# A gated pair of two-dimensional Fourier filters: a new order list, with twelve even sums moved to VectorE, late weights behind the last even F2 and seven even read-backs in a run

## Chip, cores and metric

The kernel runs on one core of a Trainium2 chip. The metric is the device time of one execution in microseconds (us). Before the change the median of three runs is 117.16 us (117.07 to 117.44).

## What is computed

The input `x` is 2048 x 1024 (S x D, bf16). Two filters A and B, each given by a real and an imaginary weight matrix of 2048 x 513, are applied in the frequency domain, and a gate for each row mixes the two results:

```python
def _A_ref(x, w_r, w_i):
    X = rfft2(x)
    X = X * (w_r + 1j * w_i)
    return irfft2(X, s=(S, D)).astype(bfloat16)
...
g = sigmoid((x * gate_w).sum(-1, keepdims=True))
a = _A_ref(x, A_w_r, A_w_i)
b = _B_ref(x, B_w_r, B_w_i)
return g * a + (1 - g) * b
```

## The kernel before

All transforms are matrix products with constant tables, and the work is cut into many small steps. Frequencies along D are split by parity: "even" units are n = 0 to 7 and "odd" units n = 8 to 15. The order of all work on all engines is written out by hand, as one list of tokens in the string `ORDER`; a token names a step, its indices, and the engine (A = ScalarE, D = VectorE, P = GpSimd, S = a transfer issued by SyncE) or, for TensorE steps, the PSUM bank (0 to 7). Each engine works through its own tokens in the order of the list; what one engine must wait for on another (data, a free PSUM bank, a free buffer) is found from the tiles that the steps touch. The last lines of the body are the whole driver:

```python
order = [tok.split(":") for tok in ORDER.split()]
for t in order:
    fn[t[0]](*t[1:])
```

The stages, with their tokens:

- `x`, `c`, `W`: loads of the input, of constants and of the weights of a unit (16 loads of 512 KB). Weights 0 to 7 lie in the tile `ro`, 8 to 11 in `wx`, and 12 to 15 in the even half of `y`, so those four must wait until the last even F2 has read `y`.
- `F1:s:par`: a first transform of input slice s (16 slices), for even (e) or odd (o) outputs; 8 matmuls. Its result is folded (sum and difference of two halves) into `y`: either `FC` copies one half to a buffer and `FD` adds and subtracts on VectorE (24 folds, line 382), or `FX` copies both and `FP` does it on GpSimd (8 folds). The buffers (`tmp`) are a ring of eight in `wx`.
- `F2:n:tt` (4 matmuls), its copy `T`; `F3:n` (12 matmuls), its copy `X`; `P:n:r`, the product with the weights on VectorE (two halves r of 2048 elements a lane, line 494); `Y`, `NA`, `N`: a small patch of one column of the even units, by TensorE and VectorE.
- `GH`, `GC`, `GT`, `GK`, `GZ`, `GS`: the gate, from GH's 32 matmuls to a sigmoid. `GW` then makes two gated tables from it in blocks of 4 (0, 4, 8, 12), with two VectorE instructions a block: `EA` = EA x E and `EB` = E - EA (lines 439 and 440).
- `J:n` (32 matmuls), copied by `R:n:r` to one of five `rl` buffers and stored by `H:n:tt` to a scratch in DRAM. `L:par:v` reads it back transposed, 512 KB each: `L:0` needs all of the even units' stores, `L:1` all of the odd units' stores. The read-backs go into `re` and `ro`.
- `V:par:v:s` (8 matmuls with EA and EB), its copy `VC`, and then for the even units `C:0:v:s` (4 matmuls). The result is copied by `EX` to a `tmp` buffer and its two halves added (h = 0) and subtracted (h = 1) by `EQ:v:s:h` into f32 rows in `re` (line 615); for unit 3, `E` copies the result as it is. For the odd units `U` (or `C:1:3`) makes the odd part, and output rows are the sum and the difference of both: `OR` on VectorE (line 635), or `OC` and `OP` by ScalarE and GpSimd (line 631), or for unit 3 `QD` and `QP` (lines 642 and 647). `S:v` stores the finished rows, whole units of 512 KB or halves.

Where a helper makes the copies, all have one line: 204 on ScalarE, 206 on VectorE.

SyncE issues all loads and stores but two, in the order of the list. A transfer that has to wait holds back all that stand behind it.

Of the kernel before, what the change touches and what calls it, by code (L numbers as in the profile page):

```python
# [10 lines left out]
P = 128  # L11
S = 2048
# [9 lines left out]


ORDER = """
warm:8 c:A:F1 c:A:gws tab:A x:S:0:1 x:S:1:1 x:S:2:2 x:S:4:2 x:S:6:2 x:S:8:2 x:S:10:2 x:S:12:2 x:S:14:2 c:S:FD:0:1
F1:1:o:0 F1:1:e:1 FX:1:o:D F1:0:o:2 FC:1:e:D F1:0:e:3 FP:1:o FD:1:e F1:3:o:0 F1:2:e:4 FC:0:e:D F1:3:e:1 gc:P FD:0:e
F1:2:o:5 FC:3:e:A FC:2:e:D F1:4:e:3 FD:3:e FX:2:o:A F1:5:o:6 FX:0:o:A FD:2:e F1:5:e:5 FC:4:e:A FP:0:o FX:3:o:A FD:4:e
F1:6:e:1 FC:5:e:A F1:4:o:2 FD:5:e FC:6:e:A F1:7:e:0 FP:2:o c:S:WF:0:4 FD:6:e F1:6:o:3 W:S:0 FC:7:e:A F1:9:e:7 FD:7:e
FX:6:o:A F1:8:e:1 FP:3:o FC:9:e:D c:S:WJ:0:4 F1:11:e:3 FD:9:e F1:10:e:0 c:S:w0 FC:11:e:A F1:7:o:4 c:S:PM FC:8:e:A
FP:6:o FD:11:e FX:5:o:A c:S:EZ F1:13:e:5 FC:10:e:A FD:8:e W:S:1 F1:12:e:6 FP:5:o FD:10:e c:S:WF:4:16 FC:12:e:A  # L30
F1:14:e:1 FC:13:e:A FD:12:e FX:4:o:A F1:15:e:3 W:S:2 F1:15:o:0 FD:13:e FP:4:o FC:15:e:A F1:11:o:2 FC:14:e:A FD:15:e
FC:15:o:A F1:8:o:6 c:S:WJ:4:16 F1:14:o:5 FD:14:e FC:8:o:A F1:10:o:3 neg:A:0:4 FD:15:o FC:14:o:A F1:12:o:7 FX:7:o:A
F2:0:0:1 FD:8:o c:S:E FC:10:o:A FP:7:o FC:12:o:A F2:1:0:0 W:S:3 FD:14:o T:0:0:A F2:0:1:4 FC:11:o:A F2:1:1:6 FD:10:o
T:1:0:A W:S:4 pw:P F1:13:o:1 T:1:1:A FD:12:o F1:9:o:0 T:0:1:A F3:1:5 FD:11:o c:S:FD:1:2 FC:9:o:A F3:0:3 FC:13:o:A
FD:9:o X:1:A W:S:5 F2:3:1:2 FD:13:o F2:2:0:7 X:0:A F2:3:0:0 P:1:0 W:S:6 Y:1:1 F2:2:1:5 T:3:0:A Y:0:3 neg:A:4:16 GH:4
P:1:1 W:S:7 T:2:0:A T:2:1:A NA:1:D N:1:D P:0:0 T:3:1:A GC:A NA:0:D P:0:1 F3:2:0 F2:4:0:5 X:2:A F2:4:1:2 F3:3:6 J:1:3:0
T:4:0:D T:4:1:A X:3:A P:2:0 Y:2:2 GT:0:5 R:1:0:A F2:5:0:6 Y:3:7 NA:2:D P:2:1 T:5:0:A H:1:0 F3:4:2 c:S:IG R:1:1:A
GT:1:5 W:S:8 F2:5:1:4 N:0:D NA:3:D P:3:0 X:4:A J:0:6:0 W:S:9 T:5:1:A H:1:1 N:2:D GT:2:5 P:3:1 R:0:0:A Y:4:2 GT:3:5
F3:5:3 W:S:10 R:0:1:A N:3:D H:0:0 F2:7:1:6 GK:D NA:4:D P:4:0 F2:6:1:2 X:5:A GZ:0:0 F2:6:0:5 P:4:1 GS:0 W:S:11 F2:7:0:7
T:7:0:A T:7:1:D J:2:3:0 T:6:0:A GW:D:4 T:6:1:A Y:5:6 GW:D:0 R:2:0:A N:4:D NA:5:D P:5:0 R:2:1:A H:2:0 W:S:12 H:0:1  # L40
P:5:1 F3:7:6 J:3:2:4 X:7:A H:2:1 F3:6:0 R:3:0:A F2:8:0:6 X:6:D F2:8:1:7 R:3:1:A F2:9:0:2 Y:7:3 T:8:0:D Y:6:0 T:8:1:A
GZ:1:4 NA:6:D T:9:0:A P:7:0 J:4:6:0 GS:1 F2:9:1:2 N:5:D P:7:1 R:4:0:A T:9:1:A H:4:0 P:6:0 J:5:4:6 W:S:13 R:4:1:A H:3:0
NA:7:D N:7:D R:5:0:A H:4:1 P:6:1 F3:8:2 F3:9:0 R:5:1:A F2:11:1:4 X:8:D F2:10:0:5 X:9:A H:5:1 F2:10:1:6 H:3:1 N:6:D
F2:11:0:7 W:S:14 P:8:0 T:10:0:A J:6:2:0 T:11:0:A T:11:1:A T:10:1:D R:6:0:A P:8:1 J:7:4:6 R:6:1:A H:6:0 F3:10:2 H:5:0
P:9:0 R:7:0:A P:9:1 R:7:1:A H:7:0 J:8:0:4 X:10:A GW:D:12 H:7:1 F2:12:0:6 H:6:1 F2:12:1:7 W:S:15 R:8:0:A T:12:0:D
P:10:0 R:8:1:A J:9:2:0 P:10:1 T:12:1:A H:8:1 F3:11:4 H:8:0 R:9:0:A F2:13:1:6 X:11:D R:9:1:A H:9:0 F3:12:2 F2:14:0:7
X:12:A H:9:1 F2:13:0:0 L:0:0 F2:14:1:1 L:0:1 T:13:0:A T:13:1:D P:11:0 L:0:2 J:10:4:2 L:0:3 T:14:0:A P:11:1 T:14:1:A
F3:13:6 R:10:0:A P:12:0 X:13:A H:10:0 J:11:0:4 L:0:4 P:12:1 R:10:1:A F3:14:6 R:11:0:A X:14:D F2:15:0:2 F2:15:1:3
T:15:0:A P:13:0 T:15:1:A J:12:0:6 R:11:1:A V:0:0:1:2 P:13:1 R:12:0:A F3:15:4 V:0:0:0:3 R:12:1:D X:15:A H:12:0
V:0:1:0:0 H:10:1 V:0:1:1:1 L:0:5 VC:0:1:0:A P:14:0 H:11:0 J:13:4:6 VC:0:0:0:A VC:0:1:1:A P:14:1 VC:0:0:1:A R:13:0:A  # L50
P:15:0 J:14:0:2 R:13:1:A H:13:0 H:11:1 C:0:0:1:4 P:15:1 H:12:1 C:0:0:0:5 EX:0:0:D R:14:0:D R:14:1:A EX:0:1:A H:14:1
J:15:6:2 H:13:1 EQ:0:1:0:P V:0:2:0:4 EQ:0:0:0:P C:0:1:1:5 R:15:0:D R:15:1:A H:14:0 C:0:1:0:0 EQ:0:0:1:P H:15:1
V:0:2:1:1 VC:0:2:0:A GW:D:8 V:0:3:1:2 H:15:0 EX:1:1:A L:0:6 V:0:3:0:3 VC:0:2:1:A EX:1:0:D L:0:7 EQ:1:1:0:P C:0:2:0:4
VC:0:3:0:D VC:0:3:1:A C:0:2:1:1 EQ:1:0:0:P V:0:4:1:0 EX:2:1:D EQ:0:1:1:P V:0:4:0:5 C:0:3:0:2 EQ:2:1:0:P VC:0:4:0:A
C:0:3:1:1 EX:2:0:A V:0:5:0:3 EQ:1:1:1:P VC:0:4:1:A V:0:5:1:5 EQ:1:0:1:P VC:0:5:0:A C:0:4:0:4 VC:0:5:1:A EQ:2:0:0:P
L:1:0 C:0:5:0:0 EX:4:0:D L:1:1 C:0:4:1:3 L:1:2 E:3:0:D EQ:4:0:0:P L:1:3 V:0:6:0:5 EX:4:1:A L:1:4 C:0:5:1:4 L:1:5
EQ:2:0:1:P VC:0:6:0:D V:0:6:1:2 L:1:6 EX:5:0:D EQ:4:0:1:P V:0:7:1:3 VC:0:6:1:A V:0:7:0:5 EX:5:1:A EQ:5:0:0:P C:0:6:0:0
L:1:7 C:0:6:1:2 EQ:2:1:1:P EX:6:1:A EQ:5:1:0:P VC:0:7:0:A VC:0:7:1:D E:3:1:D C:0:7:1:3 V:1:0:0:1 V:1:0:1:4 EQ:4:1:0:P
VC:1:0:0:A C:0:7:0:2 VC:1:0:1:D EX:6:0:A EQ:6:1:0:P U:1:0:0:1 EX:7:0:A EQ:6:1:1:P V:1:1:0:0 OC:0:0:A EQ:5:0:1:P
V:1:1:1:2 VC:1:1:0:D U:1:0:1:4 EQ:6:0:0:P V:1:2:0:5 EQ:7:0:0:P V:1:2:1:0 VC:1:2:0:A EQ:7:0:1:P U:1:1:0:1 VC:1:2:1:D  # L60
VC:1:1:1:A EQ:4:1:1:P EX:7:1:A U:1:2:0:5 OP:0:0:0 OR:0:1:1 OC:1:0:A OR:0:1:0 U:1:1:1:0 OR:2:0:0 EQ:6:0:1:P V:1:3:0:1
U:1:2:1:4 OP:0:0:1 VC:1:3:0:A V:1:3:1:2 V:1:4:0:1 OP:1:0:0 OR:1:1:0 OR:2:0:1 OR:2:1:1 S:S:0 VC:1:3:1:A OR:1:1:1
C:1:3:0:3 VC:1:4:0:A V:1:4:1:5 OR:2:1:0 EQ:7:1:0:P C:1:3:1:0 VC:1:4:1:A QD:3:0:0 S:S:2 U:1:4:0:1 OP:1:0:1 QD:3:1:1
V:1:5:0:2 QD:3:1:0 OC:4:0:A V:1:5:1:4 EQ:5:1:1:P S:S:1 VC:1:5:0:A QD:3:0:1 U:1:4:1:5 OP:4:0:0 VC:1:5:1:D U:1:5:0:0
OR:4:1:0 OP:4:0:1 U:1:5:1:1 OR:5:0:0 OR:4:1:1 V:1:7:0:4 QP:3:0:0:P V:1:6:1:2 OR:5:0:1 S:S:4 VC:1:7:0:A V:1:7:1:3
OR:5:1:1 U:1:7:0:4 VC:1:7:1:A EQ:7:1:1:P OR:5:1:0 V:1:6:0:0 QP:3:1:1:P OR:7:0:0 S:S:5 U:1:7:1:1 VC:1:6:0:A OR:7:0:1
VC:1:6:1:A QP:3:1:0:P U:1:6:0:0 S:S:7:0 OR:7:1:1 OR:7:1:0 U:1:6:1:2 QP:3:0:1:P OR:6:0:0 S:S:7:1 OR:6:1:1 OR:6:0:1
S:S:3 OR:6:1:0 S:S:6
"""


# [115 lines left out]
def gated_mix(ctx, tc, x_in, we_in, wo_in, w0_in, gw_in, out):  # L187
# [14 lines left out]
    def cp(e, out, in_):  # L202
        if e == "A":
            nc.scalar.copy(out=out, in_=in_)  # L204
        else:
            Q[e].tensor_copy(out=out, in_=in_)  # L206
# [160 lines left out]
    def tmp():  # L367
        cnt[0] += 1
        return wx[:].rearrange("p a b -> p (a b)").bitcast(F32)[:, cnt[0] % 8 * 512:cnt[0] % 8 * 512 + 512].rearrange("p (a b) -> p a b", a=2)
# [70 lines left out]
        Q[e].tensor_tensor(C["EB"][:, s], ee, C["EA"][:, s], ALU.subtract)  # L440


    def f2(n, tt, k):
        n, tt = int(n), int(tt)
        par, u = n // NU, n % NU
        ps = PS["T", n, tt] = ptile(k)
        t = 2 * u + tt
        for v in range(2):
            for b in range(2):
                nc.tensor.matmul(ps[:, v * 256:v * 256 + 256],  # L450
                                 lhsT=y[:, v, par, b, 2 * t:2 * t + 2, :, :].rearrange("p j s c -> p (j s c)"),
                                 rhs=C["FD"][:, par, v, b, :], start=(b == 0), stop=(b == 1))
# [33 lines left out]
        cp(e, X[:].rearrange("p r t m -> p t r m"), PS.pop(("X", n))[:].rearrange("p (t r m) -> p t r m", t=2, r=2))  # L486

    def prod(n, r):
        n, r = int(n), int(r)
        if r == 0:  # L490
            Ps[n] = wk.tile([P, 2, 2, 4, 256], BF16, name="p", tag="p", bufs=PB)
        X, w, p = Xs[n], Ws[n], Ps[n]
        xb = X[:, r].rearrange("p t (a m) -> p t a m", a=1).to_broadcast([P, 2, 4, 256])
        nc.vector.tensor_tensor(p[:, r], xb, w, ALU.mult)  # L494

    def parts(n, k):

# [97 lines left out]

    def even_sin(v, s, e):
        v, s = int(v), int(s)
        if ("E", v) not in TM:
            TM["E", v] = tmp()
        cp(e, TM["E", v][:, s], PS["O", 0, v, s][:, 256:512])  # L600

    def even_sum(v, s):
        v, s = int(v), int(s)
        for h, op in enumerate((ALU.add, ALU.subtract)):
            nc.vector.tensor_tensor(EV[:, v, s, 256 * h:256 * h + 256], PS["O", 0, v, s][:, 0:256], TM["E", v][:, s], op)

    def even_parts(v, s, e):
        v, s = int(v), int(s)
# [40 lines left out]
    def store(q, v, s="b"):  # L649
# [2 lines left out]
        Q[q].dma_start(ov[:, 2 * v:2 * v + 2, :][:, r], OT[v][:, r].rearrange("p s h d -> p s (h d)"))  # L652

    fn = dict(warm=warmup, x=load_x, c=load_c, W=load_w, neg=neg, gc=gate_coef, tab=table, pw=pair_weights,
              F1=f1, FG=f1g, FY=f1y, FC=f1c, FD=f1d, FX=f1x, FP=f1p, GH=gate_hat, GC=gate_copy, GT=gate_turn, GK=gate_cols, GZ=gate_z, GS=gate_s, GW=gate_weights,
              F2=f2, T=f2c, F3=f3, X=f3c, P=prod, Y=parts, NA=patch_mul, N=patch, J=i1, R=i1c, H=scratch_store, L=scratch_load, V=i2, VC=i2c, U=i3, C=i3f,
              E=even_out, ES=even_sin, EF=even_sum, EX=even_parts, EQ=even_mix, OC=odd_copy, OP=odd_pool, OR=odd_row, QD=odd_mix, QP=odd_out, S=store)
    order = [tok.split(":") for tok in ORDER.split()]
# [54 lines left out]
```

## Time and profile before

| | us |
|---|---|
| median of three runs | 117.16 (117.07 to 117.44) |
| span of the profiled execution, first to last instruction | 115.6 |
| time of the profiled execution itself | not listed; 117.16 - 115.6 = 1.56 lies around the span by the median |
| TensorE busy in matmuls | 103.6 |
| VectorE busy | 97.0 |
| ScalarE busy | 84.4 |
| GpSimd busy | 46.2 |
| moved by DMA | 36.79 MB, 318 GB/s over the span |
| mean granted TensorE clock | 0.985 |

The page gives busy time of each engine, then a row of 40 slices (2.89 us each) in tenths. Matmuls are pipelined, so a busy TensorE is not one at its peak. The `timeline` merges neighbouring instructions of one kind: a line has the start, the time covered, the engine and line, the operation with output and inputs, and how many there were. Two instructions of a kind that follow one another overlap a little in their records, so the spacing from start to start is what one costs in a full queue, and it is a little shorter than its recorded duration (for a product 1.14 against 1.215 us). DMA issues are listed with their size and the time from issue to landing.

### The profile page before, as it was taken

What the parts mean: (1) busy time and instruction counts of PE and PEld (TensorE: products, weight loads), DVE (VectorE), ACT (ScalarE), POOL (GpSimd) and SP (SyncE); (2) the same over time, 40 slices, a digit from 0 to 9 for tenths busy, and PEclk for the clock granted to TensorE, in tenths of its full rate; (3) what the DMA queues carried; (4) which work ended last, traced back from release to release, by engine and by line L of the source; (5) the groups of instructions that cost most, each with busy time, mean ns of one, the idle gap of its engine ahead of it and who ended that gap; (6) DMA issues with size and microseconds to landing.
All of it is one profiled execution on the core that took longest, in us unless ns stands there. A gap on an engine that the chain in (4) does not pass through costs nothing.

```text
span 115.6 us, 3953 instructions
## 1 busy us (share of the span) xinstructions
PE 103.6 (90%) x1619; PEld 71.3 (62%) x1619; DVE 97.0 (84%) x164; ACT 84.4 (73%) x138; POOL 46.2 (40%) x74
## 2 busy tenths in 40 slices
PE   5999999999999699898889899989979999999900
PEld 2499989875567256463445357459859765867400
DVE  0099999999999999999899999999157349999970
ACT  4009488999999999999999999977735844534300
POOL 1066995900000000000000000057986999999920
PEclk9999999999999999999999999999999999999995
DMA  3999999999579999669999999999999992482874
GB/s 90 348 326 401 403 374 367 363 397 408 210 222 324 371 394 373 169 263 397 350 293 354 348 306 401 254 357 382 352 353 411 403 418 98 198 346 119 327 279 181
DMA packets 17794, 36.79 MB, mean 318 GB/s; under 512 B 1904, under 2 KB 10736, under 8 KB 17776
## 3 DMA queue, kind: packets, MB, share of 16 engines
q1 hardware_dynamic: 17488, 36.44, 87.5%
q8 instruction: 12, 0.20, 0.6%
q10 hardware_dynamic: 288, 0.10, 0.4%
q14 instruction: 6, 0.05, 0.1%
HBM read 23.96 MB, written 12.58 MB: 316 GB/s over the span
## 4 chain that ended last, share of the span: by engine, by line
PE 39%; DVE 19%; DMA 16%; ACT 16%; issue 4%; SPq 1%; DVEq 1%; ACTq 0%
ACT rl L204 11%; PE ps L581 9%; PE ps L565 8%; DVE y L382 7%; PE ps L450 6%; PE ps L334 5%; DMA sc<-rl 5%; DMA re<-sc 4%; DMA ig<-cst_ig 4%; PE ps L537 3%; DMA re<-in_x_dram 3%; PE ps L480 3%; DVE p L494 3%; ACT X L204 3%; PE ps L590 3%
## 5 line engine op out<-in xcount | busy, mean ns | idle before, releaser
L615 POOL TENSOR_TENSOR re<-wx 128x256 f32<-128x256 f32 x28 | 19.6, 730 | 55.3 <-DMA re<-sc 53.1
L204 ACT CAST rl<-ps 128x1024 bf16<-128x1024 f32 x29 | 29.6, 1142 | 0.7 <-ACT wx L204 0.7
L204 ACT COPY wx<-ps 128x256 f32<-128x256 f32 (+1 forms) x39 | 17.2, 498 | 10.5 <-PE ps L334 8.2
L537 PE MATMUL ps<-p,wj 32*64 32x512 bf16 x512 | 20.5, 381 | 2.5 <-ACT rl L204 2.0
L204 ACT CAST V<-ps 128x512 bf16<-128x512 f32 x25 | 13.8, 601 | 11.3 <-PE ps L565 8.4
L494 DVE TENSOR_TENSOR p<-X,ro 128x2048 bf16<-128x2048 bf16 x16 | 19.1, 1215 | 0.0
L450 PE MATMUL ps<-fd,y 128*128 128x256 bf16 x128 | 16.5, 273 | 0.4 <-ACT rl L204 0.4
L382 DVE TENSOR_TENSOR y<-ps,wx 128x256 bf16<-128x256 f32 x48 | 16.4, 412 | 0.1
L334 PEld LDWEIGHTS <-re 128*128 128x128 bf16 x256 | 15.2, 100 | 1.6 <-DMA re<-in_x_dram 1.0
L334 PE MATMUL ps<-f,re 128*128 128x128 bf16 x256 | 15.8, 224 | 0.3
L204 ACT CAST T<-ps 128x512 bf16<-128x512 f32 x26 | 15.5, 693 | 0.0
L537 PEld LDWEIGHTS <-wj 32*64 32x64 bf16 x512 | 8.4, 103 | 10.6 <-issue 7.5
L382 POOL TENSOR_TENSOR y<-wx 128x256 bf16<-128x256 f32 x16 | 11.1, 734 | 8.2 <-DVE wx L206 5.9
L635 DVE TENSOR_TENSOR ot<-re,ps 128x512 bf16<-128x512 f32 x22 | 13.8, 681 | 0.4
L450 PEld LDWEIGHTS <-y 128*128 128x128 bf16 x128 | 11.5, 97 | 4.1 <-issue 2.6
L581 PE MATMUL ps<-ig,V 128*128 128x512 bf16 x56 | 13.4, 380 | 0.0
L204 ACT CAST X<-ps 128x1024 bf16<-128x1024 f32 x12 | 13.2, 1118 | 0.0
L206 DVE COPY wx<-ps 128x512 f32<-128x512 f32 (+1 forms) x10 | 5.8, 578 | 7.4 <-PE ps L334 4.8
L480 PE MATMUL ps<-T,wf 64*64 64x256 bf16 (+1 forms) x128 | 10.2, 332 | 1.1 <-DVE np L514 1.0
L590 PE MATMUL ps<-ig,V 128*128 128x256 bf16 x72 | 9.7, 273 | 0.0
L494 DVE TENSOR_TENSOR p<-X,wx 128x2048 bf16<-128x2048 bf16 x8 | 9.4, 1217 | 0.0
L494 DVE TENSOR_TENSOR p<-X,y 128x2048 bf16<-128x2048 bf16 x8 | 9.3, 1215 | 0.0
(60 smaller groups left out, 138.4 us busy)
## 6 DMA issues: line engine op xcount, KB each, us to landing
sc<-rl SPq DMA_DIRECT2D x32, 256.0 KB, 4.7
ro<-in_we_dram SPq DMA_DIRECT2D x8, 512.0 KB, 8.3
re<-sc SPq DMA_DIRECT2D x8, 512.0 KB, 6.1
ro<-sc SPq DMA_DIRECT2D x8, 512.0 KB, 7.7
re<-in_x_dram SPq DMA_DIRECT2D x7, 512.0 KB, 8.0
out_dram<-ot SPq DMA_DIRECT2D x7, 512.0 KB, 2.6
wx<-in_wo_dram SPq DMA_DIRECT2D x4, 512.0 KB, 6.6
y<-in_wo_dram SPq DMA_DIRECT2D x4, 512.0 KB, 5.0
```

Source lines behind the costliest of these rows:

```text
L204: nc.scalar.copy(out=out, in_=in_)
L334: nc.tensor.matmul(o, lhsT=lh, rhs=rh, start=(h == 0), stop=(h == 1))
L382: Q[e].tensor_tensor(yo[:, v, k:k + n, s1, :], a.rearrange("p (k c) -> p k c", c=4), b.rearrange("p (k c) -> p k c", c=4), op)
L450: nc.tensor.matmul(ps[:, v * 256:v * 256 + 256], lhsT=y[:, v, par, b, 2 * t:2 * t + 2, :, :].rearrange("p j s c -> p (j s c)"), rhs=C["FD" ...
L480: nc.tensor.matmul(view(ps[ho, tt * 512:(tt + 1) * 512], dst), lhsT=lh, rhs=view(T[hp(jh), tt, :], src), start=(w == 0), stop=(w == 1))
L494: nc.vector.tensor_tensor(p[:, r], xb, w, ALU.mult)
L537: nc.tensor.matmul(o, lhsT=lh, rhs=src[r, ri, wi, tt], start=(q == 0), stop=(q == 3))
L565: nc.tensor.matmul(ps[:, ch * 128:ch * 128 + 128], lhsT=RR[par][:, v, ch // 2, s, c0 + 256 * ab:c0 + 256 * ab + 128], rhs=Ew[:, s1, :], st ...
L581: nc.tensor.matmul(ps, lhsT=Vs[par, v][:, s, ch, :], rhs=rh, start=(ch == 0), stop=(ch == 3))
L590: nc.tensor.matmul(ps[:, o:o + 256], lhsT=Vs[par, v][:, s, ch, :], rhs=g[:, o:o + 256], start=(ch % 2 == 0), stop=(ch % 2 == 1))
L615: Q[e].tensor_tensor(EV[:, v, s, 256 * h:256 * h + 256], t[:, 0], t[:, 1], (ALU.add, ALU.subtract)[h])
L635: nc.vector.tensor_tensor(otile(v)[:, s, h, :], EV[:, v, s], PS["O", 1, v, s], (ALU.add, ALU.subtract)[h])
```

## The change

The whole list `ORDER` is replaced. Counts of tokens that differ, before and after: `FC` 4 to 1 on VectorE and 20 to 23 on ScalarE; `FX` 1 to 0 on VectorE and 7 to 8 on ScalarE; `T` 6 to 3 on VectorE, 26 to 29 on ScalarE; `X` 4 to 2 on VectorE, 12 to 14 on ScalarE; `R` 3 to 6 on VectorE, 29 to 26 on ScalarE; `EX` 5 to 6 on VectorE, 9 to 8 on ScalarE; `E` 2 to 0 on VectorE, 0 to 2 on ScalarE; `EQ` 28 to 16 on GpSimd and 0 to 12 on VectorE; `GW` becomes `GA` and `GB`, which are its two instructions as tokens of their own, four each. All TensorE steps, products, folds, loads and stores are the same in number; they stand in a new order and in part in other PSUM banks.

Places that the change names or that the text below speaks of:

- Loads: before, the constants and weights went FD, WF, W:0, WJ, ..., with W:8 and W:9 behind the first store H:1:0, and W:12 to W:15 spread between the stores. After, W:12, W:14 and W:15 go one behind the other behind the last even F2 (F2:6:1), ahead of every store; W:13 goes behind H:9:1.
- Read-backs: before, L:0:0 to L:0:3 in a run and L:0:4 to L:0:7 between and behind the odd stores. After, L:0:0, 3, 5, 1, 6, 2, 7 in a run ahead of H:8:0, and L:0:4 behind the last store H:15:0, followed by L:1:0, 3, 1, 2, 5, 6, 7, 4.
- VectorE between the last product and R:15:0: before `EX:0:0 R:14:0 R:15:0`; after `VC:0:1:1 EX:1:0 VC:0:5:0 EQ:0:0:1 GA:4 EQ:1:0:0 GB:4 R:15:0`.
- The last units: before 7 and then 6, with `S:S:6` (512 KB) last; after 6 and then 7, with `S:S:7:1` and `S:S:7:0` (256 KB each) last.

The diff, cut to its core (a few runs of the lists, and the functions):

```diff
...
-T:15:0:A P:13:0 T:15:1:A J:12:0:6 R:11:1:A V:0:0:1:2 P:13:1 R:12:0:A F3:15:4 V:0:0:0:3 R:12:1:D X:15:A H:12:0
...
-P:15:0 J:14:0:2 R:13:1:A H:13:0 H:11:1 C:0:0:1:4 P:15:1 H:12:1 C:0:0:0:5 EX:0:0:D R:14:0:D R:14:1:A EX:0:1:A H:14:1
-J:15:6:2 H:13:1 EQ:0:1:0:P V:0:2:0:4 EQ:0:0:0:P C:0:1:1:5 R:15:0:D R:15:1:A H:14:0 C:0:1:0:0 EQ:0:0:1:P H:15:1
-V:0:2:1:1 VC:0:2:0:A GW:D:8 V:0:3:1:2 H:15:0 EX:1:1:A L:0:6 V:0:3:0:3 VC:0:2:1:A EX:1:0:D L:0:7 EQ:1:1:0:P C:0:2:0:4
...
-S:S:3 OR:6:1:0 S:S:6
+R:2:0:D GZ:1:3 N:3:D R:2:1:A Y:4:2 NA:4:D P:4:0 GS:1 W:S:15 GZ:0:6 F3:7:0 Y:5:4 GA:D:8 H:1:0 GS:0 X:7:A N:4:D NA:5:D P:5:0
...
+L:0:0 L:0:3 L:0:5 L:0:1 T:14:1:A L:0:6 L:0:2 F2:14:0:1 L:0:7 J:10:2:6 T:14:0:A T:13:0:A F2:15:0:4 R:10:1:A F3:13:0 F2:15:1:7
...
+V:0:5:0:4 P:15:1 P:15:0 VC:0:1:1:D EX:1:0:D VC:0:5:0:D H:13:0 R:14:1:A H:12:0 H:13:1 H:11:1 C:0:1:1:6 V:0:5:1:7 EQ:0:0:0:P
+EQ:0:0:1:D EX:0:1:A VC:0:5:1:A GA:D:4 EX:1:1:A J:15:2:0 EQ:1:0:0:D GB:D:4 H:14:1 H:14:0 V:0:7:0:5 R:15:0:D C:0:5:0:6 R:15:1:A
+EX:5:0:A V:0:2:1:4 C:0:5:1:7 EX:5:1:A H:15:1 VC:0:2:1:D V:0:2:0:3 H:15:0 VC:0:7:0:A V:0:6:0:6 C:0:2:1:0 V:0:7:1:1 L:0:4 L:1:0
...
+EQ:2:1:0:P VC:0:3:1:A EQ:2:1:1:P EQ:5:1:0:P EQ:6:0:1:D EQ:7:0:1:D EQ:6:0:0:D EQ:6:1:0:D EQ:2:0:1:D VC:0:4:1:A C:0:3:1:0
+VC:0:4:0:A C:0:4:1:2 V:1:0:0:1 EX:4:1:A V:1:0:1:7 C:0:4:0:5 E:3:1:A VC:1:0:0:D V:1:3:1:3 EX:4:0:D E:3:0:A V:1:3:0:2
...
+    def gate_a(e, b):
+        s = slice(int(b), int(b) + 4)
+        Q[e].tensor_tensor(C["EA"][:, s], C["EA"][:, s], bc(C["E"][:]).to_broadcast([P, 4, 128]), ALU.mult)
+
+    def gate_b(e, b):
+        s = slice(int(b), int(b) + 4)
+        Q[e].tensor_tensor(C["EB"][:, s], bc(C["E"][:]).to_broadcast([P, 4, 128]), C["EA"][:, s], ALU.subtract)
```

`prod` also learns to take both halves at once (`r == "b"`), and `even_sin` and `even_sum` get buffers of their own for each half; no token of either list uses these.

## The prediction

> **What bounds the kernel now.** I read the page's busy shares and slices first, then VectorE's and SyncE's timelines, then the DMA landings around 80 us. The slices say which engine has no room in which stage:
>
> ```profile
> PE 103.6 (90%) x1619; PEld 71.3 (62%) x1619; DVE 97.0 (84%) x164; ACT 84.4 (73%) x138; POOL 46.2 (40%) x74
> ...
> PE   5999999999999699898889899989979999999900
> ...
> DVE  0099999999999999999899999999157349999970
> ACT  4009488999999999999999999977735844534300
> POOL 1066995900000000000000000057986999999920
> ...
> DMA  3999999999579999669999999999999992482874
> ```
>
> From 6 to 78 us VectorE is full, from 20 to 76 ScalarE is full, and DMA is full except for dips near 30 and 46 us. VectorE has room only from 80 to 94 us. GpSimd is busy until 23 us and from 76 us on. In the last stage TensorE and then VectorE are full. VectorE's timeline shows where the first full stretch ends and the last one begins (start, us, engine, line, what):
>
> ```profile
> 71.08 4.62 DVE L494 TENSOR_TENSOR p<-X,y 128x2048 bf16<-128x2048 bf16 x4
> 75.61 0.68 DVE L206 COPY wx<-ps 128x512 f32<-128x512 f32 x1
> 76.22 2.34 DVE L206 CAST rl<-ps 128x1024 bf16<-128x1024 f32 x2
> 78.48 0.41 DVE L439 TENSOR_TENSOR ea<-ea,e 128x512 bf16<-128x512 bf16 x1
> 78.92 0.42 DVE L440 TENSOR_TENSOR eb<-e,ea 128x512 bf16<-128x512 bf16 x1
> ...
> 94.94 5.24 DVE L635 TENSOR_TENSOR ot<-re,ps 128x512 bf16<-128x512 f32 x8
> 100.10 2.47 DVE L642 TENSOR_TENSOR pq<-re,ps 128x512 f32<-128x512 f32 x4
> ...
> 103.12 8.93 DVE L635 TENSOR_TENSOR ot<-re,ps 128x512 bf16<-128x512 f32 x14
> ```
>
> The last products (P:15) end at 75.6, the last copy out of the J stage that VectorE owns (R:15:0) at 78.5, the last output row sum at 112.05. Between the two lies one transfer chain, read from SyncE's timeline and the landings of issues from 80 to 84 us:
>
> ```profile
> 72.74 7.60 SPq L549 DMA_DIRECT2D sc<-rl  x9
> 80.40 1.44 SPq L554 DMA_DIRECT2D re<-sc  x2
> 83.95 4.47 SPq L554 DMA_DIRECT2D ro<-sc  x8
> ...
> ro<-sc SPq DMA_DIRECT2D x1, 512.0 KB, 4.8
> sc<-rl SPq DMA_DIRECT2D x1, 256.0 KB, 4.0
> ```
>
> H:15:0 (the last of the nine scratch stores) goes out at about 79.95 and lands 4.0 later, at 83.95; only then may L:1:0, the first odd read-back, go; it lands at 83.95 + 4.8 = 88.75, and TensorE's first odd matmul starts at 89.17. So the end is: last product, R:15:0, H:15:0, L:1:0, then the odd stage of 112.05 - 89.17 = 22.9 us, then the last store (115.6 - 112.05 = 3.5 us). Each edit is priced on this path.
>
> **Part 1, up to the last product.** Spacings from start to start in VectorE's timeline: product 1.14, T 0.60, X or R 1.14, fold pair 0.675, a 256-wide copy 0.34, a 512-wide one 0.61-0.68, NA or N 0.10, a gate pair 0.78. Up to P:15, before: 24 folds 16.2, 32 products 36.4, 16 NA/N 1.6, FX 0.7, 4 FC 1.4, 6 T 3.6, 4 X 4.6, 1 R 1.1, 3 gate pairs 2.4, GK 0.1: 68.0. It starts at 5.94 and ends at 75.61, so 1.7 us are lost on waits. After: the same folds, products and patches, 1 FC 0.3, 3 T 1.8, 2 X 2.3, 5 R 5.7, three gate pairs (split) 2.3, GK 0.1: 66.7, that is 1.3 less. But VectorE's first work is now behind the third F1 and not the first: 5.92 + 2 x 0.466 = 6.85, 0.9 later. And Y:0 now stands behind the 1.84 us of GH on TensorE, with NA:0 waiting for it in VectorE's queue and P:2 behind it. TensorE's list adds up to 23.2 at Y:0; at Y:1 before, it ran 5.6 behind its list, which gives 28.8; VectorE's list reaches NA:0 at 6.85 + 21.2 = 28.1. So it waits at most 0.7, less what VectorE has waited by then (a part of the 1.7): 0.3. With the old 1.7 of waits: 6.85 + 66.7 + 0.3 + 1.7 = 75.5 against 75.6. **Nothing gained** here; ends: 74.7 (half of the waits) and 77.2 (twice the waits).
>
> ScalarE gets 3 T (0.48 each), 2 X (0.91), 3 FC (0.36), 1 FX (0.47), 2 E (0.48) and loses 3 R (0.91) and one EX. From its first T to R:15:1 the lists add up to 56.5 before and 56.9 after, the added EX:0:0 and EX:1:1 included. Before, that ran from 20.45 to 78.0; so R:15:1 comes at about 78.5, still ahead of R:15:0.
>
> SyncE: the constants and weights change places; FD comes later but F2:1:0 needs FD only at 19.4 (thirty F1 of 0.466 from 4.9 on) and P:1 needs W:1 at 23. W:8 waits for the last fold (24.8), with WJ:4:16, W:6, W:9, W:7, W:10, IG and W:11 behind it: W:5 and W:3 are then still in flight. W:12, W:14, W:15 wait for F2:6:1 at about 37.5, and every H stands behind them; the first one to wait for that is R:5:0, the sixth user of five rl buffers, at about 48. In return the two dips go (SyncE stood at H:1:0 until 31.7), so weights come earlier, which nobody waits for. Cost taken: nothing.
>
> **Part 2, from the last product to the odd stage.** Between P:15 and the end of R:15:0 VectorE had EX, R:14:0, R:15:0: 0.6 + 1.15 + 1.15 = 2.9. Now it has VC, EX, VC, EQ, GA, EQ, GB, R:15:0: 3 x 0.61 + 2 x EQ + 0.36 + 0.42 + 1.14 = 3.75 + 2 EQ. No row shows an even sum (256 wide, f32, both inputs in SBUF) on VectorE; below, the 256-wide copy at 0.34; above, GpSimd's own at 0.70. I take 0.35, near the 256-wide fold half of 0.334. Sum 4.45, so R:15:0 is done at 75.5 + 4.45 = 79.95 against 78.5, and H:15:0 goes at about 80.4 against 79.95: 0.4 later. Given back by the seven read-backs in a run: ahead of L:1:0 there were L:0:6 and L:0:7, now only L:0:4, 0.52 MB less at 0.38 MB/us = 1.4 us of transfer; and the store of H:15:0 meets a shorter queue. The shortest scratch store took 2.3, this one 4.0; I take 3.2. L:1:0 then lands at 80.4 + 3.2 + 4.8 = 88.4, the odd stage starts at 88.8: **0.4 gained**, ends 1.2 gained and 1.6 lost. V:0:4, the one unit whose read-back is late, is last in TensorE's list, so the 0.8 us wait of TensorE for L:0:6 at 85.6 goes; TensorE then has 21 V and C of 0.44 = 9.3 us after J:15 (about 77.5), 86.8, and waits for L:1:0.
>
> The rest of the twelve sums, 10 x 0.35 = 3.5, and the other VectorE work behind R:15:0 until VC:1:0:0 add up to 7.0: 79.95 + 7.0 = 87, against 89.2 when V:1:0:0 is ready. They fit into the hole of 80-94 us with 2.2 to spare. GpSimd falls from 28 to 16 sums, 8.4 us less; it has 6 OP and 4 QP of 1.25 after them and is off the path.
>
> **Part 3, the tail.** Fourteen row sums (14 x 0.637 = 8.9) start after U:1:5:0. TensorE reaches its end after 12 V, 3 C and 8 U: 5.35 + 1.3 + 6.9 = 13.6. So the last row sum ends 22.5 + 0.1 after the odd stage starts, against 22.9: **0.3 gained**. The last store is half of unit 7 (256 KB, 2.0 to land) and not the whole of unit 6 (512 KB, 2.6): **0.5 gained**.
>
> Sum: 0.4 + 0.3 + 0.5 = 1.2 off the profiled span of 115.6, so 114.4. Around the span lie 117.16 - 115.6 = 1.56 by the median (the profiled execution's own time is not listed); with that, **116.0**.
>
> **Rivals.**
> (1) VectorE's sums and GpSimd's block one another, and the time is slower. VectorE's last five sums (EQ:6:0:1 to EQ:2:0:1) come while GpSimd has 2:1:0 to 7:1:1 in hand. If each of the eleven sums and gate products near R:15:0 and behind it waits for half a GpSimd sum (0.37), VC:1:0:0 is 4.0 late; 2.2 are spare, so U:1:0:0 and all of the tail move by 1.8: 116.0 + 1.8 = 117.8. It decides from 2.2 us of waits on. Against it: most of the other seven fall where GpSimd's inputs are not yet copied. The trace cannot tell: its only VectorE operations with two SBUF inputs beside GpSimd's are the gate products, 0.41 and 0.42 at 78.48 and 78.92, as long as their mean without GpSimd, but GpSimd stood idle from 78.57 to 79.17. The Trainium skill, "SBUF — State Buffer", section "Who interferes with whom", says that a VectorE instruction with two SBUF inputs and a GpSimd instruction that reads SBUF exclude one another for a whole instruction. By that rule this rival's mechanism is real and only its overlap is open; no run shown here has it.
> (2) The new middle loses more waits than the old. C:0:0:0 needs bank 3, freed by R:12:0 on VectorE behind P:14:1; J:15 stands behind V:0:5:1, which needs bank 7 from EX:1:0 behind P:15. Twice the old 1.7 us of waits gives 116.0 + 1.7 = 117.7. For it: VectorE, ScalarE and TensorE all hand over within 0.1 us here. Against it: both sums are as long as before.
> (3) The path ends at the same point: H:15 as slow as before (4.0) and the tail gains only the store: about 117.0.
> (4) The last products come 0.8 earlier and H:15:0 lands in 2.3: 114.6.
>
> **How the numbers follow.** Forecast 0.40 (115.3 to 116.8); rival 1 0.17; rival 2 0.18; rival 3 0.12; rival 4 0.13. About 0.3% (0.35 us) is what a measurement of this kernel can tell from no change. Faster 0.53, same 0.12, slower 0.35. The range takes in rival 4 and both slower ones with some spread: 114.5 to 118.4.
>
> **What would show it.** P:15 ends at 75 to 76; R:15:0 at about 80; the first odd matmul near 88.8 waits for L:1:0; VectorE's sums last 0.4 with no idle time of GpSimd behind them (rival 1: longer, or gaps); the last row sum ends 22.6 after that matmul; 3.0 from there to the end. I am wrong if P:15 ends after 77 or VC:1:0:0 after 89.5.

## The result, and the profile after

The changed kernel is slower. Twenty runs of each give medians of 118.63 us (changed) and 117.44 us (before); the ratio is 1.0085, with a 95% interval of 1.0057 to 1.0114, about 1.0 us. (The ratio leaves out executions more than 1.5% above the fastest of their kernel, so it is smaller than that of the two medians.) 116.0 was forecast. The profiled execution of the changed kernel has a span of 115.9 us and took 117.70; that is among its quicker ones.

From the page of the changed kernel, and two of its groups of instructions:

```profile
PE 102.5 (88%) x1615; PEld 69.7 (60%) x1619; DVE 101.9 (88%) x169; ACT 88.2 (76%) x145; POOL 40.0 (35%) x62
...
DVE  0099989998999999999999999999989979669990
...
L626 POOL TENSOR_TENSOR re<-wx 128x256 f32<-128x256 f32 x16 | 13.2, 847 | 60.2 <-ACT wx L201 52.2
L626 DVE TENSOR_TENSOR re<-wx 128x256 f32<-128x256 f32 x12 | 7.1, 634 | 0.1
```

VectorE's hole at 80 to 94 us has closed (9989979 in the slices where 9157349 stood). It was to take 12 sums of 0.35, 4 us in all; on the profile the twelve are busy for 7.1, 634 ns each in the mean. A sum of GpSimd (line 626 here, 615 before) takes 847 ns in the mean and not 730. VectorE's timeline from the last products on shows where that time lies:

```profile
71.53 4.23 DVE L505 TENSOR_TENSOR p<-X,y 128x2048 bf16<-128x2048 bf16 x3
...
77.48 0.57 DVE L626 TENSOR_TENSOR re<-wx 128x256 f32<-128x256 f32 x1
77.97 0.94 DVE L442 TENSOR_TENSOR ea<-ea,e 128x512 bf16<-128x512 bf16 x1
78.84 0.41 DVE L626 TENSOR_TENSOR re<-wx 128x256 f32<-128x256 f32 x1
79.17 0.94 DVE L446 TENSOR_TENSOR eb<-e,ea 128x512 bf16<-128x512 bf16 x1
80.04 1.21 DVE L203 CAST rl<-ps 128x1024 bf16<-128x1024 f32 x1
...
82.56 1.09 DVE L626 TENSOR_TENSOR re<-wx 128x256 f32<-128x256 f32 x3
...
87.62 4.23 DVE L626 TENSOR_TENSOR re<-wx 128x256 f32<-128x256 f32 x5
91.78 0.68 DVE L203 CAST V<-ps 128x512 bf16<-128x512 f32 x1
...
104.41 8.58 DVE L646 TENSOR_TENSOR ot<-re,ps 128x512 bf16<-128x512 f32 x14 [1.00 <-PE ps L592]
```

and GpSimd's timeline beside it:

```profile
73.40 1.28 POOL L626 TENSOR_TENSOR re<-wx 128x256 f32<-128x256 f32 x1 [51.51 <-ACT wx L201]
77.04 1.59 POOL L626 TENSOR_TENSOR re<-wx 128x256 f32<-128x256 f32 x2 [2.36 <-DVE wx L203]
78.85 0.98 POOL L626 TENSOR_TENSOR re<-wx 128x256 f32<-128x256 f32 x1 [0.22 <-ACT wx L201]
...
84.92 0.94 POOL L626 TENSOR_TENSOR re<-wx 128x256 f32<-128x256 f32 x1 [3.88 <-DMA re<-sc]
86.01 5.57 POOL L626 TENSOR_TENSOR re<-wx 128x256 f32<-128x256 f32 x7 [0.15 <-issue]
```

The two are to be read side by side. Three sums of VectorE at 82.56 come while GpSimd stands idle (81.0 to 84.9): 1.09 for three, 0.34 from start to start. Five at 87.62 come inside GpSimd's run of seven: 4.23, 0.85 each. The two gate products take 0.94 each beside a sum of GpSimd, where they took 0.41 and 0.42 before. And the three last products take 4.23, where three in a row take 3.49 elsewhere, just where GpSimd's first sum takes 1.28. What stands behind the five sums is VC:1:0:0, the first copy of the odd stage, at 91.78. TensorE waits for it, and at 80.17 it has waited for the second gate product (`eb`), as its waits show (engine, line, released by: us in total, times, longest):

```profile
PE ps L592 <- DVE V L203: 1.3, 1, 1.3
...
PE ps L576 <- DVE eb L446: 0.5, 1, 0.5
```

The path by stages, from the two profiles (us):

| | before | forecast | after |
|---|---|---|---|
| last product ends | 75.7 | 75.5 | 75.8 |
| R:15:0 ends | 78.5 | 79.95 | 81.25 |
| L:1:0 is issued | 83.95 | 83.6 | 84.25 |
| odd stage starts on TensorE | 89.17 | 88.8 | 88.82 |
| VC:1:0:0: VectorE is free / its input is ready; after: it starts | - | 87.0 / 89.2 | 91.78 |
| fourteen last row sums start | 103.12 | 102.5 | 104.41 |
| last row sum ends | 112.05 | 111.4 | 112.99 |
| from there to the end of the span | 3.5 | 3.0 | 2.9 |

So by the two profiles -0.4 at the start of the odd stage, +1.3 in it (24.2 against 22.9) and -0.6 at the end make the +0.3 between the spans.

### The profile page after: what moved, and what is told of

Its sections match the earlier page's. It is cut to its first block, busy times and chain, and to the rows that moved or that the text cites. A ratio compares the mean times of both kernels' runs of the same rounds, so it can differ in the third digit from the quotient of the medians.

```text
span 115.9 us, 3957 instructions
## 1 busy us (share of the span) xinstructions
PE 102.5 (88%) x1615; PEld 69.7 (60%) x1619; DVE 101.9 (88%) x169; ACT 88.2 (76%) x145; POOL 40.0 (35%) x62
## 4 chain that ended last, share of the span: by engine, by line
PE 50%; ACT 18%; DVE 12%; issue 7%; POOL 5%; DMA 4%; DVEq 1%; ACTq 0%
PE ps L576 9%; PE ps L592 9%; PE ps L455 8%; ACT rl L201 7%; PE ps L331 7%; POOL y L379 5%; PE ps L601 5%; PE ps L548 5%; DMA sc<-rl 4%; ACT T L201 4%; PE ps L485 3%; ACT X L201 3%; DVE rl L203 3%; PE ps L245 3%; ACT wx L201 2%
## 5 line engine op out<-in xcount | busy, mean ns | idle before, releaser
L626 POOL TENSOR_TENSOR re<-wx 128x256 f32<-128x256 f32 x16 | 13.2, 847 | 60.2 <-ACT wx L201 52.2
L201 ACT CAST rl<-ps 128x1024 bf16<-128x1024 f32 x26 | 26.5, 1103 | 0.6 <-PE ps L548 0.6
L201 ACT COPY wx<-ps 128x256 f32<-128x256 f32 (+1 forms) x42 | 18.5, 486 | 10.5 <-PE ps L592 4.0
L201 ACT CAST V<-ps 128x512 bf16<-128x512 f32 x25 | 14.7, 619 | 8.4 <-PE ps L576 6.0
L455 PE MATMUL ps<-fd,y 128*128 128x256 bf16 x128 | 17.7, 273 | 1.0 <-ACT rl L201 0.7
L201 ACT CAST T<-ps 128x512 bf16<-128x512 f32 x29 | 17.1, 665 | 0.1
L331 PE MATMUL ps<-f,re 128*128 128x128 bf16 x256 | 15.1, 219 | 1.1 <-ACT wx L201 1.0
L331 PEld LDWEIGHTS <-re 128*128 128x128 bf16 x256 | 14.6, 98 | 1.8 <-DMA re<-in_x_dram 1.7
L201 ACT CAST X<-ps 128x1024 bf16<-128x1024 f32 x14 | 15.3, 1091 | 0.4 <-ACT eb L201 0.3
L646 DVE TENSOR_TENSOR ot<-re,ps 128x512 bf16<-128x512 f32 x22 | 13.7, 683 | 1.9 <-PE ps L592 1.9
L485 PE MATMUL ps<-T,wf 64*64 64x512 bf16 (+1 forms) x128 | 10.0, 334 | 0.3 <-ACT rl L201 0.2
L576 PEld LDWEIGHTS <-re 128*128 128x128 bf16 x128 | 7.9, 98 | 3.5 <-issue 2.9
```

Source lines behind the costliest of these rows:

```text
L331: nc.tensor.matmul(o, lhsT=lh, rhs=rh, start=(h == 0), stop=(h == 1))
L455: nc.tensor.matmul(ps[:, v * 256:v * 256 + 256], lhsT=y[:, v, par, b, 2 * t:2 * t + 2, :, :].rearrange("p j s c -> p (j s c)"), rhs=C["FD" ...
L485: nc.tensor.matmul(view(ps[ho, tt * 512:(tt + 1) * 512], dst), lhsT=lh, rhs=view(T[hp(jh), tt, :], src), start=(w == 0), stop=(w == 1))
L576: nc.tensor.matmul(ps[:, ch * 128:ch * 128 + 128], lhsT=RR[par][:, v, ch // 2, s, c0 + 256 * ab:c0 + 256 * ab + 128], rhs=Ew[:, s1, :], st ...
L626: Q[e].tensor_tensor(EV[:, v, s, 256 * h:256 * h + 256], t[:, 0], t[:, 1], (ALU.add, ALU.subtract)[h])
L646: nc.vector.tensor_tensor(otile(v)[:, s, h, :], EV[:, v, s], PS["O", 1, v, s], (ALU.add, ALU.subtract)[h])
```

## The experiments

Theory A: an operation of VectorE with two inputs in SBUF and a sum of GpSimd hold each other up; with twelve sums and two gate products beside GpSimd's sums, VectorE is late for the odd stage (rival 1 of the prediction). Theory B: the new middle loses the time (rival 2). C: VectorE just has too much work. D: such a sum costs 0.85 by itself. Ratios are to the kernel before, measured beside it, with 95% intervals; 5 rounds each. The changed kernel was not measured again beside the experiments, so a comparison with its 1.0085 is one between two series. In the experiments the even sum has line 624, 625 or 611.

**Five sums later.**

```diff
-... EX:6:0:D ... EQ:6:0:1:D EQ:7:0:1:D EQ:6:0:0:D EQ:6:1:0:D EQ:2:0:1:D ... VC:1:0:0:D ... EX:4:0:D ... VC:1:3:1:D
+... EX:6:0:D ... VC:1:0:0:D ... EX:4:0:D ... VC:1:3:1:D EQ:2:0:1:D EQ:6:0:1:D EQ:7:0:1:D EQ:6:0:0:D EQ:6:1:0:D
```

> The five even sums 2:0:1, 6:0:1, 7:0:1, 6:0:0, 6:1:0 stay on VectorE but stand behind VC:1:3:1 in its queue, not ahead of VC:1:0:0. In the changed kernel they took 87.62 to 91.85 us (0.85 each) and VC:1:0:0 began at 91.78, 2.0 us after V:1:0:0 was done. Theory A (the sums and GpSimd's sums exclude one another, and what hurts is that the odd stage's first copy queues behind them): VC:1:0:0 begins by 90.0, U:1:0:0 by 91.0, the last row sum 1.0 to 1.8 earlier than in the changed kernel; ratio to the kernel before 0.993 to 1.000. Theory B (the new order loses its time in the middle, before the last product): ratio stays at 1.006 to 1.011. Theory C (VectorE simply has more work and is the bound to the end, wherever the sums stand): the sums come out of the row sums' idle time only in part, ratio 1.003 to 1.008.

Ratio 1.0156 (1.0091 to 1.0221). VC:1:0:0 began at 90.02, as A expected, but the rest of A's numbers missed. VectorE's timeline:

```profile
90.02 0.69 DVE L202 CAST V<-ps 128x512 bf16<-128x512 f32 x1 [1.94 <-PE ps L575]
...
92.09 4.58 DVE L625 TENSOR_TENSOR re<-wx 128x256 f32<-128x256 f32 x5
96.60 1.27 DVE L652 TENSOR_TENSOR pq<-re,ps 128x512 f32<-128x512 f32 x2
```

The five still take 0.9 each beside GpSimd, now ahead of the odd rows (QD, line 652), which hold PSUM banks; TensorE waited 2.7 us for those. At both places the sums are dear, because GpSimd works there; the move only chose who waits.

**Gate products earlier.** `GA:D:4` and `GB:D:4` directly behind `GB:D:12`.

> GA:4 and GB:4 (two inputs in SBUF) move from behind the last product, where they took 0.94 each beside GpSimd's sums, to behind GB:12, where GpSimd has nothing. Theory A (exclusion): both take 0.42 there, the last product ends 0.7 to 0.8 later, R:15:0 ends 0.9 to 1.1 earlier than 81.25; VC:1:0:0 is that much earlier; ratio 0.6 to 0.9% lower than the changed kernel's 1.0085. If these two are slow for another reason (their operands at this place): 0.94 each in the new place, R:15:0 unchanged, ratio 1.0085.

Ratio 1.0012 (0.9977 to 1.0046), 0.7% under the changed kernel, as A says. Both took 0.42 there, R:15:0 ended 4.3 after the last product, not 5.5, and TensorE's wait of 0.5 for the second gate product went.

**Without GpSimd's sums.**

```diff
-    all sixteen tokens EQ:...:P
```

> Leaves out the sixteen even sums of GpSimd, so these halves of the even rows are not made and the output is not the reference's; the twelve sums of VectorE stay where they are. Theory A (exclusion): VectorE's sums cost 0.33 to 0.35 each in a run (recorded 0.41), GA:4 and GB:4 0.42 each, the products of unit 15 1.14; VC:1:0:0 2 to 3 us earlier than 91.78; ratio 0.975 to 0.99. Theory D (an f32 sum of two SBUF inputs costs 0.85 on VectorE by itself): the five still take 4.2 us, and the ratio stays within 0.3% of 1.0085 except for what follows from free buffers.

Ratio 0.9941 (0.9903 to 0.9980), above the span of ratios that A gave. VectorE's operations themselves:

```profile
78.66 0.42 DVE L440 TENSOR_TENSOR ea<-ea,e 128x512 bf16<-128x512 bf16 x1
...
79.33 0.42 DVE L444 TENSOR_TENSOR eb<-e,ea 128x512 bf16<-128x512 bf16 x1
...
87.50 1.77 DVE L624 TENSOR_TENSOR re<-wx 128x256 f32<-128x256 f32 x5
89.44 0.69 DVE L201 CAST V<-ps 128x512 bf16<-128x512 f32 x1 [0.17 <-PE ps L574]
```

The same five sums, in the same place: 1.77 and not 4.23. D falls: with GpSimd silent the price is 0.34 from start to start, the 0.35 of the forecast. VC:1:0:0 now waits for TensorE. C falls as the main cause as well: VectorE has the same work here, and the ratio is 1.4% lower. But with the sixteen sums more is gone than their blocking: GpSimd's later operations and their buffers come free too, so this ratio is not the price of the blocking alone.

**All three moves together.** The moves of the first two, and `EQ:0:0:0:P` behind `EQ:1:0:1:P`.

> The changes of e1 and e2 together, and GpSimd's first sum (0:0:0) behind 1:0:1, so that it cannot fall into the products of unit 15 (in the changed kernel it took 1.28 there and a product 0.74 more than its 1.14). Theory A: P:15 ends within 0.2 of 75.7 although GA:4 and GB:4 are ahead of it, R:15:0 ends at 79.4 to 79.9, the odd stage begins at 88.0 to 88.8, VC:1:0:0 right behind; the last row sum at 110.0 to 111.2; ratio 0.980 to 0.993, faster than the kernel before. Theory B: ratio not under 1.003.

Ratio 0.9993 (0.9939 to 1.0046): not the gain that A expected, and not told apart from the kernel before. It carries the first experiment's bad place of the five sums: in its profile they take 4.58, and TensorE waits the same 2.7 us.

**The twelve sums alone, in the old order.** In the list before, the same twelve `EQ` tokens with D for P.

> The kernel before, with one part of the change alone: the same twelve even sums go to VectorE, at the places their tokens have in the old list; nothing else differs. Theory A (exclusion between GpSimd's sums and VectorE's operations with two SBUF inputs): the sums of VectorE that fall beside GpSimd's take 0.7 to 0.9 each, those beside an idle GpSimd 0.33; the odd stage's copies (VC:1) queue behind them; ratio 1.000 to 1.015. Theory C (only VectorE's added work of 12 x 0.34 counts, and it fits into the hole of 80 to 94 us): ratio 0.990 to 1.000.

Ratio 1.018 (1.0118 to 1.0242), even above A's span. VectorE's sums among the odd rows, and GpSimd's work there:

```profile
93.38 1.92 DVE L611 TENSOR_TENSOR re<-wx 128x256 f32<-128x256 f32 x2
...
102.91 1.50 DVE L611 TENSOR_TENSOR re<-wx 128x256 f32<-128x256 f32 x1
```

```profile
93.56 2.87 POOL L627 TENSOR_TENSOR ot<-re,wx 128x512 bf16<-128x512 f32 x2
...
102.86 2.67 POOL L627 TENSOR_TENSOR ot<-re,wx 128x512 bf16<-128x512 f32 x2 [2.84 <-issue]
```

Beside GpSimd's longer operation OP (1.28 by itself) one sum takes 1.50. By the ratios this part of the change costs more by itself than the whole change. By the profile, 1.3 us of it lie behind the last product (37.6 from there to the last row sum, 36.4 in the kernel before); the last product itself came 0.7 later, with the same list up to there.

**One input from PSUM.** As the second experiment, and VectorE's six late sums are made by `ES` and `EF`, which take one operand from the PSUM bank:

```diff
-EX:2:0:D EQ:2:0:0:D ... EX:6:1:A EX:6:0:D ... EQ:6:0:1:D EQ:7:0:1:D EQ:6:0:0:D EQ:6:1:0:D EQ:2:0:1:D ... EQ:6:1:1:P
+ES:2:0:D EF:2:0 ... ES:6:1:A EF:6:1 ES:6:0:D EF:6:0 ... EQ:7:0:1:P
```

> As e2, and VectorE's six late sums are those of the units 2:0, 6:0 and 6:1, made from the PSUM bank and a copied half, so that each has one input in SBUF; GpSimd has sixteen sums as before, among them 7:0:1. Theory A (only two SBUF inputs exclude GpSimd): the six cost 0.33 to 0.35 each beside GpSimd's run, VC:1:0:0 begins 2.0 to 3.0 earlier than e2's 91.21, the ratio falls 1.0 to 1.6% under e2's 1.0012. Theory E (any VectorE operation beside GpSimd's sums is held up, or the bank held longer stalls TensorE as much): no lower than e2 by 0.3%.

Ratio 0.9978 (0.9941 to 1.0014). VectorE's sums (line 615) and, in the second fence, GpSimd's run beside them:

```profile
87.11 0.76 DVE L615 TENSOR_TENSOR re<-ps,wx 128x256 f32<-128x256 f32 x2 [0.28 <-ACT wx L200]
...
88.23 0.76 DVE L615 TENSOR_TENSOR re<-ps,wx 128x256 f32<-128x256 f32 x2
89.83 0.69 DVE L202 CAST V<-ps 128x512 bf16<-128x512 f32 x1 [0.84 <-PE ps L575]
```

```profile
85.21 5.99 POOL L625 TENSOR_TENSOR re<-wx 128x256 f32<-128x256 f32 x8 [2.91 <-ACT wx L200]
```

Four sums inside GpSimd's run of eight take 0.34 from start to start, and VC:1:0:0 waits for TensorE again, not for VectorE. For a single sum this is the direct test of A: the same neighbour, the same f32 sum, and one input in PSUM. (For the time it is less direct: these sums also stand at other places, and the copies ahead of them are half as long.) By the Trainium skill ("SBUF — State Buffer", "Who interferes with whom") an operation of VectorE with at most one SBUF input, outside the modes that use two ports, does not contend with GpSimd; the runs agree, 0.34 against 0.85. From the last product to the last row sum this kernel needs 34.5 us, the second experiment 36.3, the changed kernel 37.2. The ratio fell by only 0.34%, with intervals that overlap, and not by A's 1.0 to 1.6%; in the profiled execution the last product came 0.9 later than in the second experiment's.

**GpSimd's first sum out of the last products.** As the second experiment, with `EQ:0:0:0:P` behind `EQ:1:0:1:P`.

> As e2, and GpSimd's first sum (0:0:0) stands behind 1:0:1, so that it comes after the products of unit 15 (in e2 they took 4.02 for three, against 3.49 elsewhere). Theory A: the three take 3.49, R:15:0 0.3 to 0.6 earlier than in e2, ratio 0.2 to 0.5% under e2's 1.0012. If the product is only late for another reason: 4.0 again.

Ratio 1.0026 (0.9992 to 1.0059), not lower. The three products took 3.49, as A says, so they too had been held up by GpSimd; but R:15:0 ended 4.3 after them as before, and TensorE waited 0.9 for L:1:0. This collision was real, and no cost of it shows in the time.

**All sums on GpSimd, in the new order.** The twelve tokens with P for D.

> The changed kernel with all 28 sums on GpSimd again, in the order of the list. Theory A: VectorE's VC:1:0:0 begins by 89.6 and U:1:0:0 by 90.6, but GpSimd has 12 x 0.70 = 8.4 us more and its sums 4:1:0 to 4:1:1 and products of the odd rows come later; its queue ends at 114 to 116 against 108.5, so that unit 4 and 3 are late and the ratio is 1.01 to 1.05: the move of the sums is then worth its cost in this order. If GpSimd had room, the ratio is 0.995 to 1.003.

Ratio 1.0167 (1.0119 to 1.0214). VC:1:0:0 began at 89.03, but GpSimd summed without a break:

```profile
80.78 16.49 POOL L625 TENSOR_TENSOR re<-wx 128x256 f32<-128x256 f32 x24 [2.54 <-ACT wx L200]
```

and VectorE's row sums waited 3.2 for its sum 4:1:1. Its queue ended at 110.2, not 114 to 116. So with all sums on GpSimd the new order is slower still than the changed kernel (the intervals do not meet): taking twelve away is right here, and the loss is where they went.

**Clear of GpSimd, and sooner.** As "one input from PSUM", with `EQ:0:0:0:P` behind `EQ:1:0:1:P`, and `EQ:0:0:1:D EQ:1:0:0:D` behind `R:15:0:D`.

> As e6, with GpSimd's first sum behind 1:0:1 (as in e7) and VectorE's sums 0:0:1 and 1:0:0 behind R:15:0, which then waits only for J:15. Theory A, continued (with the blocking gone, the chain R:15:0, H:15:0, L:1:0 sets the odd stage's start): the three last products take 3.49, R:15:0 ends 1.0 to 1.6 sooner after P:15 than in e6 (4.3 there), L:1:0 is issued and the odd stage starts 0.5 to 1.2 sooner; ratio 0.985 to 0.993. If TensorE or the copies, and not the read-back, set the start of the odd stage: ratio within 0.3% of e6's 0.9978.

Ratio 0.9918 (0.9874 to 0.9962): faster than the kernel before. The expected way was not it: R:15:0 waited 1.16 for J:15 and ended 4.2 after the last product, and from the last product to the last row sum it took 34.5 as in the sixth experiment, whose interval overlaps. In its profile the last product came 0.7 earlier than in that one's. Its gain over that one is not settled.

**The read-backs alone, in the old order.**

```diff
-L:0:3 H:10:0 L:0:4 ... L:0:5 ... H:15:0 ... L:0:6 ... L:0:7
+L:0:3 L:0:4 L:0:5 L:0:6 H:10:0 ... H:15:0 L:0:7
```

> The kernel before with one part of the change alone: L:0:4, L:0:5 and L:0:6 directly behind L:0:3, so that seven even read-backs stand in a run ahead of H:10:0, and L:0:7 behind H:15:0. The forecast gave this part 0.4 us of gain: TensorE's wait of 0.8 for L:0:6 at 85.6 goes and L:1:0 is issued 0.3 to 0.8 sooner; ratio 0.992 to 0.998. If the odd stores are held up behind the read-backs by as much (they wait in SyncE's queue and for the free places of eight outstanding transfers): ratio 0.999 to 1.006.

Ratio 1.0044 (1.0000 to 1.0088): no gain. TensorE's wait for a read-back in the even stage went, but the odd stores came later, one of them so late that R:15:0 waited for its buffer:

```profile
78.35 1.23 DVE L202 CAST rl<-ps 128x1024 bf16<-128x1024 f32 x1 [0.79 <-DMA sc<-rl]
```

L:1:0 was issued at 84.83, 0.9 later than before, and yet TensorE's odd stage started at 88.98, 0.2 earlier: here it did not hang on L:1:0.

**The weights spread again.** In the changed kernel `W:S:14` behind `H:3:1` and `W:S:15` behind `H:6:1`.

> The changed kernel with one part undone: W:14 behind H:3:1 and W:15 behind H:6:1, not ahead of all stores. The forecast gave this part nothing: ratio within 0.3% of the changed kernel's 1.0085, and the last product at 75.3 to 76.5. If the early weights held up the stores and the rl buffers: ratio 0.998 to 1.005, with ScalarE's R copies sooner.

Ratio 1.0124 (1.0067 to 1.0181); the last product at 76.4. The interval overlaps that of the changed kernel: no cost of the early weights is shown. (In its profile the gate products happened to fall beside an idle GpSimd and took 0.41 each, but L:1:0 went out only at 85.30 and TensorE waited 1.1 for a read-back; from the last product to the last row sum it took 37.0.)

**The last store whole.** One `S:S:7` for the two halves.

> The changed kernel with one store of 512 KB for unit 7 at the end in place of two of 256 KB. The forecast gave the halves 0.5: from the end of the last row sum to the end of the span 3.4 to 3.6 and not 2.9; ratio 1.011 to 1.015. If only the last half's size counts little: 2.9 to 3.1, ratio 1.0085.

From the last row sum to the end 3.6, not 2.9: the halves save 0.7. The ratio, 1.0212 (1.0161 to 1.0263), is higher than that explains; the last product came at 76.8 in its profile, 1.1 later, though nothing ahead of it differs. Most of that lies at one place, inside the step F2:6:1, where TensorE stands still between two matmuls; the changed kernel's profile first, then this one's:

```profile
37.98 0.38 PE L455 MATMUL ps<-fd,y 128*128 128x256 bf16 x2 [0.28 <-issue]
```

```profile
39.06 0.38 PE L454 MATMUL ps<-fd,y 128*128 128x256 bf16 x2 [1.06 <-issue]
```

The profile names nothing that released it. Of the eleven profiles with the changed order up to here, eight have this wait, of 0.28 to 1.06, and three have none; the three profiles with the old order have no such wait of TensorE. In the eight a load of 16 KB on the DMA queue for instructions had ended 1.3 to 1.6 us before TensorE went on; whether that is the cause was not tested.

## Why the prediction was wrong, step by step

- Last product at 75.5: measured 75.8. The number is right, in part by luck. VectorE's first work came at 5.90 and not at 6.85, and behind it 3.2 us were lost on waits and blocking, not 2.0: Y:0 behind GH made NA:0 wait 0.6 (0.3 was taken), and GpSimd's first sum held up the last three products by 0.7, for which the sum has no term. In the profiles with the old order up to there the last product ended at 75.7, 75.8 and 76.4, in those with the changed order 75.8, 76.2, 76.2, 76.4, 76.5 and 76.8. So theory B, rival 2, is neither shown nor ruled out: the medians differ by 0.5, and the wait in F2:6:1 is found in the new order alone.
- R:15:0 at 79.95: measured 81.25. **The step that failed first is "3.75 + 2 EQ" with 0.35 for a sum and 0.36 and 0.42 for the gate products.** The sums took 0.49 and 0.33, the gate products 0.87 each from start to start, because GpSimd had sums in hand; the third experiment, without those, has 0.34 for all four.
- Odd stage at 88.8: measured 88.82, but not on the path of the forecast, which has TensorE done with the even work at 86.8 and waiting for L:1:0. L:1:0 was issued at 84.25 and landed 4.1 later, at 88.35, and no wait of TensorE for it shows. TensorE's even work itself ran up to 88.82: J:15 ended at 78.6 and not at 77.5, and TensorE stood 0.5 for the second gate product, which GpSimd had held up. So the right number is luck. (The kernel before shows no wait of TensorE for L:1:0 either: that landed at 88.75, the odd stage started at 89.17.) The 0.4 of gain put down to the read-backs in a run was not found when that part stood alone.
- **"They fit into the hole of 80-94 us with 2.2 to spare": here the forecast fell.** With 0.85 for each of the last five and R:15:0 late, VectorE was free for VC:1:0:0 at 91.8 and not at 87.0, 4.8 later, more than twice the 2.2; after 89.5 was the prediction's own sign of being wrong. TensorE waited 1.3 for that copy. The fourteen last row sums began 15.6 after the start of the odd stage, against 13.7 as forecast. That 1.9 is close to rival 1 as it was priced: 4.0 of waits, 2.2 spare, 1.8 lost. It had a chance of 0.17. The mechanism and its price were on paper; what was misjudged is its chance. That the price came so near is in part luck: it was put together from eleven delays of 0.37, and the runs show two gate products and five sums with about 0.5 each. The twelve sums do fall mostly into GpSimd's idle time (seven of the twelve took 0.3 to 0.5), but the five that do not stand directly ahead of the copy on which the tail hangs.
- Last store: 0.6 saved by the profiles, 0.7 by the last experiment, 0.5 forecast. Right.
- What is settled, and what stays open: single operations show that VectorE and GpSimd hold each other up. The same sum takes 0.85 beside GpSimd's sums, 0.34 with GpSimd silent and 0.34 with one input in PSUM. What it is worth on the path is read from the last product to the last row sum: 36.4 us before, 37.2 in the changed kernel, 36.3 with the gate products out of the way, 34.5 with the late sums' input in PSUM as well. The ratios go the same way, and the two that lie below 1 with all of their interval (0.9941, 0.9918) are of kernels without the blocking of the late sums; but each of them differs in other things too. Open is the rest of the loss: the two profiled spans differ by 0.3, the kernels by the ratio by about 1.0. The profiled execution of the changed kernel has the earliest last product of the six with its order and the shortest of the eight waits in F2:6:1, so the rest may well lie there; the runs do not settle it.

## What to carry to other kernels

Before work is moved from GpSimd to VectorE, look at where the inputs lie: with both in SBUF the price here was VectorE's own time plus a good part of GpSimd's operation (0.85 for a sum of 0.34 beside GpSimd's sums, 1.50 beside an operation of 1.28), and it is paid by whatever stands next in VectorE's queue. Use a form with one input from PSUM where there is one, or a time when GpSimd is truly empty. An estimate of "spare time" in a hole holds only until the first instruction behind the hole that others wait for: sum up to that instruction, not over the hole. And where the path is said to wait for a transfer, look in the waits whether the engine really stands still for it: a landing just before a start is no proof.

## What the runs showed of the hardware

Not only the f32 sums are held up by GpSimd: bf16 gate products (0.94 against 0.42) and bf16 products of 2048 elements (three in 4.23 against 3.49) are as well, and GpSimd's sum in turn took 1.28 beside a product and 0.73 without. Beside GpSimd's operations of 1.28, one VectorE sum took 1.50. A VectorE sum with one input in PSUM was not slowed at all (0.34).
